# Sliding-window attention and an MLP on one core: key and value tiles 64 tokens off the query tiles

## The chip, the cores and the metric

The kernel runs on one core of one Trainium2 chip. The metric is the device time of one execution in microseconds. Three executions of the kernel before took 310.89, 311.5 and 312.32 us (median 311.5).

## The reference

Eight batches of eight heads, 576 tokens, head size 64. Each query sees itself and the 127 tokens before it, with a bias that falls linearly with the distance (ALiBi). Then comes a layer norm, an MLP with 2048 hidden units, and a residual. All inputs and the output are float32.

```python
window = 128
scores = scale * np.matmul(q, k.transpose(0, 1, 3, 2))
bias = slopes[:, None, None] * (-np.abs(rel).astype(np.float32))[None, :, :]
mask = (rel >= 0) & (rel < window)
scores = np.where(mask, scores + bias[None], -1000000000.0)
attn = softmax(scores)                      # max taken off, sum + 1e-9
x = np.matmul(attn, v)                      # -> (batch, seq, 512)
xn = (x - mu) / np.sqrt(var + 1e-06) * g_ln
out = x + np.maximum(xn @ w_ch1, 0.0) @ w_ch2
```

## The kernel before

**Blocks.** The batches are taken in four pairs (p = 0 to 3). A pair has nine blocks of 128 queries: blocks 0 to 7 are 128-token tile i = blk // 2 of batch blk % 2, and block 8 (T, the tail) holds the last 64 tokens of both batches. Block n of the whole order is p * 9 + blk, 36 in all.

**Attention of a block.** `load_qk` and `load_v` fetch queries, keys and values with POOL's DMAs, which turn float32 into float16. `turn` brings queries and keys into head-size-on-rows form: for pair 0 and the first two tiles of pair 1 with TensorE transposes (L304) and copies on DVE and ACT, from tile (1, 2) on with SP's DMA transposes (L325). Query rows are put in an order of evens first, which `store` undoes with two DMAs (L936) for each block. `attend` (L412) makes the scores with keys as the stationary side: for each pair of heads hp, each key tile (the block's own and the one before) and each head j, two products with 64 keys each in 64x64 tiles of the array (L439). `seen` cuts them to the queries that see anything, so that of two products one has 128 columns and the other 64. Four heads go to one of the two score buffers (two banks each, one for each j). ACT takes the exponential of the whole buffer, seen or not (L448, 128x1024), and DVE multiplies with a mask that holds the decay (L459; `m_full` for ordinary blocks, `m_ends` and `m_tail` for the tail, which is scored by two calls and a third, `scores_tail`). `values` multiplies the weights with the values in full 128x128 products of 65 columns (L492: 64 values and a column of ones for the sum), four heads to a bank, and divides (L500, L501).

**From block to MLP.** `stats` (DVE, POOL) and `normal` (L531) give a centred and scaled block, which SP's DMA transpose (L539) turns into `xT`. Groups of two blocks (the first six) and of four (the last six) pass `mlp1` (L740, evictions with ReLU on ACT, L756) and `mlp2` (L773) or, from group 6 on, `fast_mlp2` (L839), which uses seven products of quarters instead of eight, with sums made by DVE.

**Order.** The order on every engine is written out by hand. `steps` is a list of attention work: for block n >= 8, values of n, scores of n + 2, then statistics and masks, loads up to block n + 8, and turns of a later tile. `weave_at` runs the units of an MLP product and puts the next steps behind the units whose numbers it is given; the kernel's end lists them for each group. PE, ACT, DVE, POOL and SP each work through their own queue in that order. `decay` fills a mask with eight exponentials on ACT (L119). The products of MLP, values and turns share four PSUM banks, which from group 6 on are a `ring`.

Of the kernel before, what the change touches and what calls it, by code (L numbers as in the profile page):

```python
# [27 lines left out]

NV = 10
BY_DMA_TURN = (1, 2)  # L30
AHEAD = 8
# [8 lines left out]
def distances():  # L40

    key = np.arange(P)[:, None]
    query = np.arange(P)[None, :]

    def far(rel, ok=True):
        return np.where(ok & (rel >= 0) & (rel < WINDOW), rel, FAR)

    ends = [far(P + query - HALF * b - key, query // HALF == b) for b in range(2)]
    tail = far(query - key, query // HALF == key // HALF)
    evens_first = np.r_[0:P:2, 1:P:2]
    both = [far(P + query - key), far(query - key)]
    cols = [m[:, evens_first] for m in both] + [*ends, tail]
    return np.concatenate(cols, axis=1).astype(np.float16)


@with_exitstack
def kernel(  # L60
# [21 lines left out]
    def pool(name, bufs, **kw):  # L82
# [18 lines left out]
    dist_dram = nc.inline_tensor(distances(), name="distances")  # L101
    dist = consts.tile([P, 5 * P], FP16)
    nc.sync.dma_start(out=dist, in_=dist_dram.ap())
# [23 lines left out]
    nc.sync.dma_start(out=g_sb, in_=moe_g_ln.rearrange("(kb p) -> p kb", p=P))  # L127
    QF, QD = NFB // 2, DM // 2
    hsum = [consts.tile([P, QF, 2 * P], FP16, name=f"hs{i}", tag=f"hs{i}") for i in range(2)]
    g_line, g_row = (  # L130
        t.rearrange("p f d -> p (f d)")[:, 0 : 2 * DM].bitcast(FP32) for t in hsum
    )
    g_line = g_line[0:1]
# [75 lines left out]

    def by_dma(p, i):  # L210
        return (p, i) >= BY_DMA_TURN

    def load_qk(src, tag, p, i):

        n = min(P, S - i * P)
        t = raw_pool.tile([P, H, 2, D], FP16, tag=tag, name=tag)
        raw[tag, p, i] = t
        if by_dma(p, i):
            t = raw[tag, p, i] = t.rearrange("p h r d -> p (h r d)").rearrange(
                "p (b h d) -> p b h d", b=2, h=H  # L220
            )
            for b in range(2):
                rows = src[2 * p + b, :, i * P : i * P + n, :]
                if i == 4:
                    parts = [(t[b * n : (b + 1) * n, 0], rows)]
                elif tag == "k":
                    parts = [(t[:, b], rows)]
                else:
                    rows = rows.rearrange("h (c r) d -> h r c d", r=2)
                    parts = [  # L230
                        (t[r * HALF : (r + 1) * HALF, b], rows[:, r]) for r in range(2)
                    ]
                for dst, part in parts:
                    nc.gpsimd.dma_start(out=dst, in_=part.rearrange("h p d -> p h d"))  # L234
            return
        for b in range(2):
# [7 lines left out]
    def load_v(p, blk):  # L244
        vx = vext[(p * NSLOT + blk) % NV]
        for b, t0, n, p0 in spans(p, blk):
            nc.gpsimd.dma_start(  # L247
                out=vx[p0 : p0 + n, :, 0:D],
                in_=v[b, :, t0 : t0 + n, :].rearrange("h p d -> p h d"),
            )  # L250
# [6 lines left out]
    for n, (p, blk) in enumerate(order):  # L257
        for src, tag in ((q, "q"), (k, "k")):
            sooner = tag == "q" and 0 < blk < T and by_dma(p, blk // 2)
            if blk % 2 == 0 and not sooner:  # L260
                loads.append((load_qk, src, tag, p, blk // 2))
# [48 lines left out]
    def turn(p, i, in_sc=False, copies=(nc.vector.tensor_copy, nc.scalar.copy)):  # L310
# [3 lines left out]


        k = keys_tile("k", p, i)
        q = queries(p, i) if i < 4 else keys_tile("q", p, i)
        if by_dma(p, i):
            for tag, dst in (("q", q), ("k", k)):
                src = raw.pop((tag, p, i))  # L320
                for b in range(2 if i < 4 else 1):
                    t = dst[:, b]
                    if tag == "q" and i < 4:
                        t = turned["q", p, i][:, b].rearrange("p h r c -> p h (r c)")
                    nc.sync.dma_start_transpose(  # L325
                        out=t, in_=src[:, b].rearrange("p h d -> p (h d)")
                    )
            return
        ps = [bank(b if in_sc else None) for b in range(2)]
# [21 lines left out]
    def queries(p, i):  # L351
        if by_dma(p, i):
            t = turned_pool.tile([P, 2, HP, 2, HALF], FP16, tag="q", name="q")
            turned["q", p, i] = t
            return t
        t = turned_pool.tile([P, 2, 2, HP, HALF], FP16, tag="q", name="q")
        turned["q", p, i] = t.rearrange("p b r h c -> p b h r c")
        return t

    def keys_tile(tag, p, i):  # L360
        t = turned_pool.tile([P, 2, HP, P], FP16, tag=tag, name=tag)
        turned[tag, p, i] = t
        return t
# [34 lines left out]
    def seen(p, blk, o, t, whole):  # L398


        both, every = slice(0, 2), slice(0, HALF)
        first, second = slice(0, HALF // 2), slice(HALF // 2, HALF)
        if whole or p == 0 and blk < SEEN:
# [51 lines left out]

    def masks(p, blk, n=3):
# [21 lines left out]
    def values(p, blk, hg):  # L478
# [10 lines left out]
        for i in range(4):  # L489
            h = 4 * hg + i  # L490
            for n, (pr, t, o) in enumerate(terms):
                nc.tensor.matmul(  # L492
                    ps[:, i, :],
                    pr[:, h, t, :],
                    vext[(p * NSLOT + o) % NV][:, h, :],
                    start=(n == 0),
                    stop=(n == len(terms) - 1),
                )
        rec = small.tile([P, 4], FP32, tag="rec", name="rec")
        nc.vector.reciprocal(out=rec, in_=ps[:, :, D])  # L500
# [133 lines left out]
    def scores_step(n):  # L634
        return [(scores,) + order[n]]
# [4 lines left out]
    def values_steps(n):  # L640
        p, blk = order[n]
        return [
            [(masks, p, blk), (values, p, blk, 0)],
# [283 lines left out]
    def store(p, blk, o, cols=slice(0, DM), queues=(nc.sync,)):  # L927
        queues = cycle(queues)
        for b, t0, w, p0 in spans(p, blk):
            dst, src = out[b, t0 : t0 + w, cols], o[p0 : p0 + w, cols]  # L930
            if blk == T:
                next(queues).dma_start(out=dst, in_=src)
# [25 lines left out]
    with tc.manual_schedule(engines={engine.PE, engine.SP, engine.Pool}):  # L958
        with tc.manual_schedule(engines={engine.Activation, engine.DVE}):
# [52 lines left out]
```

## Time and profile before

| what | value |
|---|---|
| median of three runs | 311.5 us |
| the profiled execution | 308.64 us |
| its span, first to last instruction | 306.9 us |
| scores L439, products | 1088: 568 of 128 columns, 520 of 64 |
| values L492, products | 544, 65 columns, mean 193 ns |
| MLP L740, products of 512 columns | 384, mean 379 ns |
| granted TensorE clock | 0.999 |

PE is the profile's TensorE, PEld its weight loads; DVE, ACT, POOL and SP are the vector, scalar, GpSimd and sync engines. A product's own duration in the profile runs from its start to a modelled end and overlaps with the next ones: 512 columns are given 379 ns, but 32 of them, from 136.59 to 143.51 us, take 216 ns each. So what a group of products costs is read from the start of the group to the start of the next one.

### The profile page before, as it was taken

To read this page: it belongs to the slowest core of one execution; us is meant where nothing else is said; L and a number is where in the kernel's file an instruction comes from. 1 tells how busy PE (TensorE), PEld (TensorE's weight loads), DVE (VectorE), ACT (ScalarE), POOL (GpSimd) and SP (SyncE) were. 2 spreads that over 40 slices of the span, in tenths; PEclk is the share of its full clock that TensorE was granted. 3 is DMA by queue.
4 is the path that set the end of the run, shared out by engine and by line. 5 is a ranking of instruction groups with operands and counts; after the bars stand their busy time and mean duration, and the time that the engine had idled before them with its cause. 6 is when DMAs were issued, how large, how long until landed. Compare 5 with 4: busy or idle time off the path is not lost.

```text
span 306.9 us, 9072 instructions
## 1 busy us (share of the span) xinstructions
PE 297.2 (97%) x3747; PEld 200.5 (65%) x3747; DVE 220.6 (72%) x533; ACT 171.2 (56%) x297; POOL 150.6 (49%) x210
## 2 busy tenths in 40 slices
PE   8989999999999999899999999999999999999994
PEld 2468755766858576445875687568656865784583
DVE  2679877868696887737994799479948984761363
ACT  7588774757748467278247724772486257305600
POOL 8933658682399988617685657517310231000001
PEclk9999999999999999999999999999999999999999
DMA  9999999999999999999999999998845062025004
GB/s 111 159 207 201 188 167 170 202 116 117 112 100 162 149 146 139 169 151 150 88 141 183 211 88 138 134 204 65 126 88 106 17 129 47 18 45 111 0 2 137
DMA packets 150843, 38.28 MB, mean 125 GB/s; under 512 B 141809, under 2 KB 146417, under 8 KB 150802
## 3 DMA queue, kind: packets, MB, share of 16 engines
q0 software_dynamic: 103808, 18.49, 89.2%
q1 hardware_dynamic: 46594, 18.76, 37.3%
q8 instruction: 29, 0.48, 0.7%
q10 hardware_dynamic: 400, 0.46, 0.5%
q14 instruction: 12, 0.10, 0.1%
HBM read 36.90 MB, written 9.44 MB: 151 GB/s over the span
## 4 chain that ended last, share of the span: by engine, by line
PE 88%; ACT 4%; DVE 4%; DMA 3%; issue 0%; DVEq 0%
PE ps_r L740 27%; PE ps_r L839 24%; PE ps_m L773 12%; PE ps_m L740 10%; PE ps_sc L439 5%; PE ps_r L492 3%; DMA xT<-xc 3%; ACT probs L448 2%; PE ps_pv L492 2%; PE ps_warm L286 2%; PE ps_sc L304 1%; DVE o L857 1%; PE ps_tx L584 1%; DVE x L501 1%; PE ps_tr L304 0%; ACT k L337 0%
## 5 line engine op out<-in xcount | busy, mean ns | idle before, releaser
L740 PEld LDWEIGHTS <-w1g 128*128 128x128 f16 x640 | 61.0, 98 | 49.8 <-issue 2.9
L740 PE MATMUL ps_r<-xT,w1g 128*128 128x512 f16 x384 | 84.8, 379 | 1.3 <-DMA xT<-xc 1.3
L448 ACT ACTIVATE probs<-ps_sc 128x1024 f16<-128x1024 f32 x56 | 54.2, 1026 | 56.0 <-PE ps_sc L439 56.0
L756 ACT ACTIVATE ht<-ps_r 128x512 f16<-128x512 f32 x96 | 56.1, 599 | 33.3 <-PE ps_r L740 33.1
L544 POOL TENSOR_TENSOR rstd<-moments,powers 128x1 f32<-128x1 f32 x28 | 14.1, 502 | 93.2 <-DVE moments L590 93.2
L773 PE MATMUL ps_m<-w,ht 128*128 128x512 f16 x192 | 45.5, 380 | 0.0
L839 PE MATMUL ps_r<-w,ht 128*128 128x256 f16 x384 | 43.9, 273 | 0.0
L839 PEld LDWEIGHTS <-ht 128*128 128x128 f16 x384 | 37.2, 98 | 4.7
L247 POOL DMA_DIRECT2D vx<-in_v_dram x40 | 34.9, 879 | 8.3 <-DVE probs L459 2.1
L756 ACT ACTIVATE ht<-ps_m 128x256 f16<-128x256 f32 x91 | 33.3, 389 | 7.5 <-PE ps_m L740 4.6
L459 DVE TENSOR_TENSOR probs<-probs,m 128x1024 f16<-128x1024 f16 x56 | 35.7, 675 | 2.0 <-ACT probs L448 2.0
L234 POOL DMA_DIRECT2D q<-in_q_dram x46 | 31.8, 702 | 2.4 <-DMA q<-in_q_dram 1.1
L740 PE MATMUL ps_m<-xT,w1g 128*128 128x256 f16 x256 | 30.4, 273 | 0.7 <-ACT ht L756 0.6
L773 PEld LDWEIGHTS <-ht 128*128 128x128 f16 x192 | 17.3, 98 | 18.0
L589 DVE BATCH_NORM_STATS2 st<-x 128x6 f32<-128x512 f16 x36 | 24.8, 688 | 0.7
L547 POOL TENSOR_TENSOR rstd<-rstd,powers 128x1 f32<-128x1 f32 x28 | 22.7, 812 | 2.2
L500 DVE RECIPROCAL rec<-ps_r 128x4 f32<-128x4 f32 x36 | 6.3, 176 | 23.9 <-PE ps_r L492 23.8
L234 POOL DMA_DIRECT2D k<-in_k_dram x26 | 22.3, 867 | 0.6 <-PE ps_m L740 0.5
L839 PE MATMUL ps_r<-w,hs 128*128 128x256 f16 x192 | 21.9, 273 | 0.0
L492 PEld LDWEIGHTS <-probs 128*128 128x128 f16 x448 | 18.7, 97 | 4.6 <-DVE probs L459 0.3
L439 PE MATMUL ps_sc<-q,k 64*64 64x128 f16 (+1 forms) x1088 | 19.9, 208 | 1.5 <-ACT probs L448 1.0
L857 DVE TENSOR_TENSOR o<-ps_r,o 128x512 f32<-128x512 f32 (+1 forms) x25 | 16.6, 666 | 5.5 <-PE ps_r L839 5.1
(87 smaller groups left out, 359.0 us busy)
## 6 DMA issues: line engine op xcount, KB each, us to landing
out_dram<-o SPq DMA_DIRECT2D x66, 128.0 KB, 4.2
k<-in_k_dram POOLq DMA_DIRECT2D x32, 128.0 KB, 6.3
vx<-in_v_dram POOLq DMA_DIRECT2D x32, 128.0 KB, 8.1
w<-in_moe_w_ch_dram POOLq DMA_DIRECT2D x8, 512.0 KB, 11.2
q<-in_q_dram POOLq DMA_DIRECT2D x48, 64.0 KB, 6.6
q<-in_q_dram POOLq DMA_DIRECT2D x12, 128.0 KB, 4.7
k<-in_k_dram POOLq DMA_DIRECT2D x8, 64.0 KB, 5.2
vx<-in_v_dram POOLq DMA_DIRECT2D x8, 64.0 KB, 4.5
```

The source lines that it names most:

```text
L234: nc.gpsimd.dma_start(out=dst, in_=part.rearrange("h p d -> p h d"))
L247: nc.gpsimd.dma_start(out=vx[p0 : p0 + n, :, 0:D], in_=v[b, :, t0 : t0 + n, :].rearrange("h p d -> p h d"),)
L439: nc.tensor.matmul(in_halves(ps[cols, j, n, t, :])[:, r, queries], kt[rows, hp, cols], in_halves(qt[rows, b, hp])[:, r, queries], start=Tr ...
L448: nc.scalar.activation(out=dst.rearrange("p (n j) q -> p j n q", j=2), in_=ps.rearrange("p j n t q -> p j n (t q)"), func=AF.Exp, scale=in ...
L459: nc.vector.tensor_tensor(out=dst, in0=dst, in1=mask, op=ALU.mult)
L492: nc.tensor.matmul(ps[:, i, :], pr[:, h, t, :], vext[(p * NSLOT + o) % NV][:, h, :], start=(n == 0), stop=(n == len(terms) - 1),)
L547: nc.gpsimd.tensor_tensor(out=here, in0=here, in1=powers[:, 1:2], op=ALU.pow)
L589: nc.vector.bn_stats(out=st, in_=xs[order[n]])
L740: nc.tensor.matmul(ps[:, 0:cols], w[:, kb, fb * P : (fb + 1) * P], xT[:, kb, 0:cols], start=(kb == 0), stop=(kb == NKB - 1),)
L756: nc.scalar.activation(out=ht[:, fb, 0:cols], in_=ps[:, 0:cols], func=AF.Relu)
L773: nc.tensor.matmul(sums[at], ht[:, fb, at * P : (at + 1) * P], w2[:, fb, :], start=(fb == 0), stop=(fb == NFB - 1),)
L839: nc.tensor.matmul(banks[name][pair][:, pair, :], lhs[:, fb, pair * P : (pair + 1) * P], rhs[:, fb, :], start=(first and fb == 0 and (pair ...
```

## The change

From pair 1 on (`LATE = 1`):

- Key and value tiles begin 64 tokens off the query tiles: tile 0 holds tokens 0 to 63 of a batch, tile i tokens 128 i - 64 to 128 i + 63. All 128 queries of a tile see some part of the middle tile; the first half of the queries sees also the second half of the tile before, and the second half the first half of the tile after. The window thus is one 128x128 piece and two 64x64 corners. `FIRST_ROWS` and `LAST_ROWS` are the two halves of the rows, `BEYOND` the columns 128 to 191.
- `attend_late` makes the corners with 64x64 tiles (64 queries) and the middle piece with 64x128 tiles (128 keys, 128 queries); four heads fill 768 columns instead of 1024. Block T is scored in two calls instead of three, and `scores_tail` is left for pair 0 alone.
- `values_late` takes the eight heads together: first the middle piece of all, then the corners, added into the same sums; then `divide`, which is the old end of `values`.
- Every tile of the late pairs is turned by DMA, keys one tile ahead of queries; queries stay in their natural order, so a tile's queries are loaded with two DMAs instead of four and a block is stored with one instead of two.
- A new mask `m_late`, filled by `decay` in the middle of `mlp1(2)`, serves all late blocks; `m_full` and `m_ends` share the memory of `hsum`. There are 12 value tiles instead of 10, five turned key tiles instead of four, three turned query tiles instead of four.
- The places of the steps in `mlp1(5)` change.

```diff
-NV = 10
-BY_DMA_TURN = (1, 2)
+NV = 12
+LATE = 1
...
+    low, high = key < HALF, key >= HALF
+    outer = far(np.where(low, query - key, query + P + HALF - key), query < HALF)
+    cols += [far(query + HALF - key), outer[:, :HALF]]
...
-    m_full, m_ends = (
-        consts.tile([P, H, 2 * P], FP16, name=f"m{i}", tag=f"m{i}") for i in range(2)
-    )
+    QF, QD = NFB // 2, DM // 2
+    hsum = [consts.tile([P, QF, 2 * P], FP16, name=f"hs{i}", tag=f"hs{i}") for i in range(2)]
+    m_full, m_ends = hsum
+    m_late = consts.tile([P, H, P + HALF], FP16)
...
+            t0 = i * P - HALF * (tag == "k" and i > 0)
+            half = i == (0 if tag == "k" else 4)
-                rows = src[2 * p + b, :, i * P : i * P + n, :]
-                if i == 4:
-                    parts = [(t[b * n : (b + 1) * n, 0], rows)]
-                elif tag == "k":
-                    parts = [(t[:, b], rows)]
+                if half:
+                    dst, n = t[b * HALF : (b + 1) * HALF, 0], HALF
                 else:
-                    rows = rows.rearrange("h (c r) d -> h r c d", r=2)
-                    parts = [
-                        (t[r * HALF : (r + 1) * HALF, b], rows[:, r]) for r in range(2)
-                    ]
-                for dst, part in parts:
-                    nc.gpsimd.dma_start(out=dst, in_=part.rearrange("h p d -> p h d"))
+                    dst, n = t[:, b], P
+                nc.gpsimd.dma_start(
+                    out=dst, in_=heads_last(src[2 * p + b, :, t0 : t0 + n, :])
+                )
...
+    def v_at(p, o):
+        return vext[(p * NSLOT + o + max(p - LATE, 0)) % NV]
+
+    def load_v(p, o):
+        vx = v_at(p, o)
+        if p < LATE:
+            parts = spans(p, o)
+        elif o < 2:
+            parts = [(2 * p + o, 0, HALF, HALF)]
+        else:
+            parts = [(2 * p + o % 2, o // 2 * P - HALF, P, 0)]
...
+        i, odd = divmod(blk, 2)
+        late = p >= LATE
+        if not odd:
+            if not late or i == 0:
+                loads.append((load_qk, q, "q", p, i))
+            if not late or blk < T:
+                loads.append((load_qk, k, "k", p, i + late))
+            if blk == T and LATE <= p + 1 < NPAIR:
+                loads.append((load_qk, k, "k", p + 1, 0))
         loads.append((load_v, p, blk))
-        if blk % 2 and blk < T - 1 and by_dma(p, blk // 2 + 1):
-            loads.append((load_qk, q, "q", p, blk // 2 + 1))
+        if late and blk == T:
+            loads.append((load_v, p, T + 1))
+        if late and odd:
+            loads.append((load_qk, q, "q", p, i + 1))
...
+            todo = [("q", p, i)] + [("k", p, i + 1)] * (i < 4)
+            if (i == 0 and p == LATE) or (i == 4 and p + 1 < NPAIR):
+                todo.append(("k", p + (i == 4), 0))
+            for tag, p, i in todo:
+                src, dst = raw.pop((tag, p, i)), keys_tile(tag, p, i)
+                for b in range(1 if i == (0 if tag == "k" else 4) else 2):
+                    nc.sync.dma_start_transpose(
+                        out=dst[:, b], in_=src[:, b].rearrange("p h d -> p (h d)")
+                    )
+            return
...
+        t = turned_pool.tile([P, 2, 2, HP, HALF], FP16, tag="q", name="q", bufs=3)
+            [P, 2, HP, P], FP16, tag=tag, name=tag, bufs=3 if tag == "q" else 5
...
-        if o == blk:
-            return [(0, both, every), (1, both, second)]
-        return [(1, both, every), (0, both, first)]
...
+    def key_tile(p, b, o):
+        t = turned["k", p, o]
+        return t[:, 0, :, b * HALF : (b + 1) * HALF] if o == 0 else t[:, b]
+    def attend_late(p, blk, hps):
+        i, b = divmod(blk, 2)
+        heads = slice(2 * hps[0], 2 * hps[-1] + 2)
+        width = 2 * P if blk == T else P if i == 0 else P + HALF
+        if hps[0] == 0:
+            if i == 0:
+                pr = own_pool.tile([P, H, 1, P], FP16, tag="own", name="own")
+            else:
+                pr = probs_pool.tile([P, H, 2, P], FP16, tag="probs", name="probs")
+            pr = pr.rearrange("p h t q -> p (h t q)")[:, 0 : H * width]
+            weights_of[p, blk] = pr = pr.rearrange("p (h c) -> p h c", h=H)
+        else:
+            pr = weights_of[p, blk]
+        at = len(scored) % 2
+        scored.append((p, blk))
+        ps = ps_sc[at][:, :, 0 : len(hps) * width].rearrange("p j (n c) -> p j n c", c=width)
+        qt = turned["q", p, i]
+        def products(part):
+            for n, hp in enumerate(hps):
+                for dst, col, o, keys, bq, queries in part:
+                    for j in range(2):
+                        rows = slice(j * HALF, (j + 1) * HALF)
+                        nc.tensor.matmul(
+                            ps[dst, j, n, col : col + queries.stop - queries.start],
+                            key_tile(p, bq, o)[rows, hp, keys],
+                            qt[rows, bq if blk < T else 0, hp, queries],
+                            start=True,
+                            stop=True,
+                        )
+        every, low, high = slice(0, P), FIRST_ROWS, LAST_ROWS
+        if blk == T:
+            mine = [(c, slice(c * HALF, (c + 1) * HALF)) for c in range(2)]
+            outer = [(high, P + c * HALF, 3, high, c, qs) for c, qs in mine]
+            inner = [(every, c * HALF, 4, every, c, qs) for c, qs in mine]
+        elif i == 0:
+            outer = [(low, 0, 1, low, b, high)]
+            inner = [(high, 0, 0, low, b, every)]
+        else:
+            outer = [(high, P, i - 1, high if i > 1 else low, b, low)]
+            outer += [(low, P, i + 1, low, b, high)]
+            inner = [(every, 0, i, every, b, every)]
+        products(outer)
+        products(inner)
+        dst = pr[:, heads]
+        nc.scalar.activation(
+            out=dst.rearrange("p (n j) c -> p j n c", j=2),
+            in_=ps,
+            func=AF.Exp,
+            scale=inv_sqrt_d,
+        )
+        m = m_late[:, heads]
+        if blk == T:
+            todo = [
+                (
+                    dst[:, :, x * P : (x + 1) * P].rearrange("p h (b c) -> p h b c", b=2),
+                    m[:, :, x * P : x * P + HALF].unsqueeze(2).broadcast_to([P, 4, 2, HALF]),
+                )
+                for x in range(2)
+            ]
+        elif i == 0:
+            todo = [(dst[high], m[high, :, 0:P]), (dst[low, :, 0:HALF], m[low, :, BEYOND])]
+        else:
+            todo = [(dst, m)]
+        unmasked.setdefault((p, blk), []).extend(todo)
...
+        if p >= LATE:
+            for hps in [every] if blk < 2 else [low, high]:
+                attend_late(p, blk, hps)
...
+    def values_late(p, blk):
+        n = p * NSLOT + blk
+        if n % 2 == 0:
+            x_pairs[n // 2] = x_pool.tile([P, 2, DM], FP16, tag="x", name="x")
+        xs[p, blk] = x_pairs[n // 2][:, n % 2, :]
+        i, b = divmod(blk, 2)
+        pr = weights_of.pop((p, blk))
+        every, low, high = slice(0, P), FIRST_ROWS, LAST_ROWS
+        if blk == T:
+            mine = [slice(c * HALF, (c + 1) * HALF) for c in range(2)]
+            inner = [(qs, every, qs, T + c) for c, qs in enumerate(mine)]
+            outer = [
+                (qs, high, slice(P + c * HALF, P + (c + 1) * HALF), T - 2 + c)
+                for c, qs in enumerate(mine)
+            ]
+        elif i == 0:
+            inner = [(every, high, every, b)]
+            outer = [(high, low, slice(0, HALF), 2 + b)]
+        else:
+            inner = [(every, every, every, blk)]
+            outer = [(low, high, BEYOND, blk - 2), (high, low, BEYOND, blk + 2)]
+        ps = [
+            psum("ps_pv")[:, 0 : 4 * (D + 1)].rearrange("p (h d) -> p h d", h=4)
+            for _ in range(2)
+        ]
+        for part in (inner, outer):
+            for hg in range(2):
+                for h in range(4):
+                    for dst, keys, queries, o in part:
+                        nc.tensor.matmul(
+                            ps[hg][dst, h, :],
+                            pr[keys, 4 * hg + h, queries],
+                            v_at(p, o)[keys, 4 * hg + h, :],
+                            start=part is inner and h == 0,
+                            stop=part is outer,
+                            skip_group_check=True,
+                        )
+        for hg in range(2):
+            divide(p, blk, hg, ps[hg])
+    def divide(p, blk, hg, ps):
...
+        if p >= LATE:
+            return [[(masks, p, blk), (values_late, p, blk)], []]
...
-    steps += [values_steps(6)[1], x_step(6) + masks_of(7), variance_of(5)]
+    steps += [values_steps(6)[1], x_step(6) + masks_of(7), variance_of(5) + [(decay, m_late, 5)]]
     steps += [*values_steps(7), x_step(7) + variance_of(6)]
-    steps += [turn_step(8) + variance_of(7), scores_step(8) + turn_step(9)]
+    steps[-1] += turn_step(9)
+    steps += [turn_step(8) + variance_of(7), scores_step(8) + turn_step(11)]
...
-            if by_dma(order[m][0], order[m][1] // 2) == (m == n + 4)
+            if (order[m][0] >= LATE) == (m == n + 4)
-    steps.append(turn_at(8))
+    steps.append([])
-        if n + 1 < count and order[n + 1][1] == T:
-            step += [(scores_tail, order[n][0])]
...
-            if blk == T:
+            if blk == T or p >= LATE:
...
-            weave_at(mlp1(5), 0, 5, 5, 8, 10, 12, also=(3, 6, 9))
+            weave_at(mlp1(5), 0, 4, 4, 6, 8, 10, also=(3, 7, 11))
```

More of the change, by code (lines that the diff above doesn't have):

```diff
@@ L101 @@
     dist_dram = nc.inline_tensor(distances(), name="distances")
-    dist = consts.tile([P, 5 * P], FP16)
+    dist = consts.tile([P, 6 * P + HALF], FP16)
     nc.sync.dma_start(out=dist, in_=dist_dram.ap())
@@ L127 @@
     nc.sync.dma_start(out=g_sb, in_=moe_g_ln.rearrange("(kb p) -> p kb", p=P))
[L128 to L132, printed above, removed]
+    spread = hsum[1].rearrange("p f d -> p (f d)").bitcast(FP32)
+    g_line, g_row = spread[:, 0:DM], spread[:, DM : 2 * DM]
     g_line = g_line[0:1]
@@ L208, with heads_last @@
     raw = {}
-    def by_dma(p, i):
-        return (p, i) >= BY_DMA_TURN
+    def heads_last(rows):
+        return rows.rearrange("h p d -> p h d")
     def load_qk(src, tag, p, i):
-        n = min(P, S - i * P)
         t = raw_pool.tile([P, H, 2, D], FP16, tag=tag, name=tag)
         raw[tag, p, i] = t
-        if by_dma(p, i):
+        if p >= LATE:
             t = raw[tag, p, i] = t.rearrange("p h r d -> p (h r d)").rearrange(
@@ L242, in load_qk @@
             )
-    def load_v(p, blk):
-        vx = vext[(p * NSLOT + blk) % NV]
-        for b, t0, n, p0 in spans(p, blk):
+    def v_at(p, o):
[8 more added lines that the diff above has]
+            parts = [(2 * p + o % 2, o // 2 * P - HALF, P, 0)]
+        for b, t0, n, p0 in parts:
             nc.gpsimd.dma_start(
-                out=vx[p0 : p0 + n, :, 0:D],
-                in_=v[b, :, t0 : t0 + n, :].rearrange("h p d -> p h d"),
+                out=vx[p0 : p0 + n, :, 0:D], in_=heads_last(v[b, :, t0 : t0 + n, :])
             )
@@ L257 @@
     for n, (p, blk) in enumerate(order):
[L258 to L261, printed above, removed]
+        i, odd = divmod(blk, 2)
[7 more added lines that the diff above has]
+                loads.append((load_qk, k, "k", p + 1, 0))
         loads.append((load_v, p, blk))
-        if blk % 2 and blk < T - 1 and by_dma(p, blk // 2 + 1):
-            loads.append((load_qk, q, "q", p, blk // 2 + 1))
+        if late and blk == T:
+            loads.append((load_v, p, T + 1))
+        if late and odd:
+            loads.append((load_qk, q, "q", p, i + 1))
         place.append(len(loads))
@@ L310, in turn @@
     def turn(p, i, in_sc=False, copies=(nc.vector.tensor_copy, nc.scalar.copy)):
+        if p >= LATE:
[9 more added lines that the diff above has]
+            return
         k = keys_tile("k", p, i)
         q = queries(p, i) if i < 4 else keys_tile("q", p, i)
[L318 to L328, printed above, removed]
         ps = [bank(b if in_sc else None) for b in range(2)]
@@ L360, in keys_tile @@
     def keys_tile(tag, p, i):
-        t = turned_pool.tile([P, 2, HP, P], FP16, tag=tag, name=tag)
+        t = turned_pool.tile(
+            [P, 2, HP, P], FP16, tag=tag, name=tag, bufs=3 if tag == "q" else 5
+        )
         turned[tag, p, i] = t
@@ L402, in seen @@
         first, second = slice(0, HALF // 2), slice(HALF // 2, HALF)
-        if whole or p == 0 and blk < SEEN:
+        if whole or blk < SEEN:
             return [(0, both, every), (1, both, every)]
@@ L454, in attend @@
         unmasked.setdefault((p, blk), []).append((dst, mask[:, heads, :]))
-    def masks(p, blk, n=3):
+    FIRST_ROWS, LAST_ROWS = slice(0, HALF), slice(HALF, P)
+    BEYOND = slice(P, P + HALF)
+    def key_tile(p, b, o):
[65 more added lines that the diff above has]
+        unmasked.setdefault((p, blk), []).extend(todo)
@@ L457, in masks @@
+    def masks(p, blk, n=4):
         todo = unmasked.get((p, blk), [])
@@ L463, in scores @@
         low, high, every = [0, 1], [2, 3], [0, 1, 2, 3]
-        if blk == T:
+        if p >= LATE:
+            for hps in [every] if blk < 2 else [low, high]:
+                attend_late(p, blk, hps)
+        elif blk == T:
             attend(p, T, [6, 7], m_ends, "probs", low)
```

12 lines of the change are left out of this document (5 added, 7 removed).

## The prediction

> **What bounds the kernel now.** I read the page first (span, busy shares, chain), then the stages, then TensorE's instructions in order of time, where the starts of neighbouring groups give prices that the mean durations hide.
>
> ```profile
> span 306.9 us, 9072 instructions
> PE 297.2 (97%) x3747; PEld 200.5 (65%) x3747; DVE 220.6 (72%) x533; ACT 171.2 (56%) x297; POOL 150.6 (49%) x210
> PE 88%; ACT 4%; DVE 4%; DMA 3%; issue 0%; DVEq 0%
> ```
>
> PE is busy for 97% of the span and is 88% of the chain. The busy time of each engine by stage:
>
> ```profile
> 75.00:129.00 54.00, 51.93 (x713) 36.28 (x707) 42.12 (x101) 32.56 (x63) 40.93 (x56) 1.00 1.64 138
> 129.00:245.00 116.00, 116.00 (x1356) 79.24 (x1355) 90.21 (x198) 64.57 (x93) 55.21 (x76) 1.00 1.44 126
> ```
>
> From 129 us on PE (second figure) is never idle, with DVE at 90.2 and ACT at 64.6 of 116 us. So whatever PE issues more or less there goes into the time one for one, and work saved on the other engines goes nowhere. Before 129 us there are a few waits. PE in order of time, in four places of the dense stages (start, duration, line, tiles, count):
>
> ```profile
> 151.33 0.65 PE L492 MATMUL ps_r<-vx,probs 128*128 128x65 f16 x16
> 151.91 0.54 PE L439 MATMUL ps_sc<-q,k 64*64 64x128 f16 x32
> 152.39 1.92 PE L839 MATMUL ps_r<-w,w 128*128 128x256 f16 x16
> ...
> 182.21 0.45 PE L439 MATMUL ps_sc<-q,k 64*64 64x64 f16 x32
> 182.58 0.28 PE L839 MATMUL ps_r<-w,w 128*128 128x256 f16 x1
> ...
> 256.54 0.32 PE L439 MATMUL ps_sc<-q,k 64*64 64x64 f16 x16
> 256.79 0.39 PE L740 MATMUL ps_r<-xT,w1g 128*128 128x512 f16 x1
> ...
> 263.70 0.23 PE L492 MATMUL ps_r<-vx,probs 128*128 128x65 f16 x2
> ...
> 264.43 0.82 PE L839 MATMUL ps_r<-w,ht 128*128 128x256 f16 x6
> ```
>
> Start to start: the 24 value products at 263.70 hand over to another 128x128 product after 0.73 us, 30.4 ns each. The 16 at 151.33 should take 0.487, but the 64x64 scores start after 0.58: **0.093 us goes into the change of tile shape**. Scores of 64 columns take 0.25 for 16 and 0.37 to 0.38 for 32, so 16 cost 0.126 (four in 31.5 ns) and about 0.125 is fixed: 0.025 for a slower first four, 0.10 for the change back. A visit to 64x64 tiles thus costs 0.12 going in and 0.10 coming out. An ordinary block (2 to 7) costs 0.58 + 0.48 = 1.06 us, in two changes of shape.
>
> **The change on PE.** The late pairs have 27 blocks: 18 ordinary, 6 first ones (blocks 0 and 1) and 3 tails. I write X for a change between two small shapes (64x64 with 64x128 or 128x64), which no row shows.
>
> Ordinary block, before: 32 score products, half of 128 columns, half of 64. After: 16 corners of 64 columns in 64x64 (four side by side, 31.5 ns) and 8 of 128 columns in 64x128. Per set of heads that is 192 columns in both versions, so no streaming is saved. The values go from 16 products to 8 full ones and 16 corners in 64x64. After: own keys 8 x 30.3 ns = 0.242; change 0.12; corners as 8 pairs x 31.5 ns = 0.252; scores twice (corners 2 x 31.5 ns = 0.063, full keys 2 x 56 ns = 0.112), the 56 being half of the 109 ns between L740's starts with 256 columns; change back 0.10. Sum 1.07 + 3X: corners to full keys, to corners, to full keys. Against 1.06: +0.012 + 3X, times 18: **+0.2 + 54X**.
>
> First blocks: values were 8 products (0.24, and 0.12 to go to the scores); now 8 of 64x128 in one row half, then 8 corners in a single quarter: 0.12 + 0.242 + X + 0.252, so +0.24 + X. Scores have the same 16 products, but corners and own keys now share half of the array and run after one another, 4 x 31.5 + 4 x 56 = 0.35 instead of 0.22: +0.1. Times 6: **+2.0 + 6X**.
>
> Tails: scores 0.606 + 3X against 0.354, and the 16 of the tail (0.126, in the last pair 0.25 with its own changes) go away; values 16 of 128x64 in pairs and 16 corners in pairs, 0.744 against 0.845 (in the last pair 0.1 more for the way out). Over the three: **+0.3 + 9X**.
>
> Turns: two turns by PE (L304, 64 products each) leave, 0.69 and 0.88 us from the starts around 67.5 and 72.3 us: **-1.6**.
>
> So PE gets +0.97 + 69X. **X** is bounded below by 0 (the rows of the array stay in halves of 64) and above by 0.12 (going in from 128x128). I take 0.093, the bare handover measured at 151.91, as the nearest row: 69 x 0.093 = 6.4.
>
> The Trainium skill, TensorEngine Tiling (Array Packing), Key Properties, says that a change of tiling mode, not of the tile alone, drains TensorE; 64x64 and 64x128 are different modes in its list. The 0.093 us agrees for 128x128 to 64x64, and no run here shows the other pairs. By that rule X is not 0, which speaks against this change.
>
> **The other engines.** On the path only before 129 us:
>
> ```profile
> L448 ACT ACTIVATE probs<-ps_sc 128x1024 f16<-128x1024 f32 x56 | 54.2, 1026 | 56.0 <-PE ps_sc L439 56.0
> L756 ACT ACTIVATE ht<-ps_r 128x512 f16<-128x512 f32 x96 | 56.1, 599 | 33.3 <-PE ps_r L740 33.1
> L119 ACT ACTIVATE m<-dist 128x256 f16<-128x256 f16 x16 | 5.1, 408 | 1.0 <-DMA dist<-distances 1.0
> 111.63 2.34 PE L740 MATMUL ps_m<-xT,w1g 128*128 128x256 f16 x20 [0.29 <-ACT ht L756]
> 128.86 0.81 PE L740 MATMUL ps_r<-xT,w1g 128*128 128x512 f16 x3 [1.32 <-DMA xT<-xc]
> ```
>
> Exponentials: 768 instead of 1024 elements. Busy over count is 0.97 us for 1024 and 0.58 for 512, so 0.78: 0.39 less per block. Behind them PE lost time three times: the stretches of L740 from 97.74, 109.42 and 114.77 take 2.65, 4.39 and 3.57 us where 109 ns each make 2.18, 3.92 and 3.05: 0.47 + 0.47 + 0.52 = 1.46. Most of 0.39 comes back each time: **-1.15** (bounds -1.46 and 0).
>
> The wait at 128.86: the last piece of xT is issued by SP at 120.97 and lands 7.75 us later (chain). The new weave puts its block two units earlier, SP has one store less per block, and PE has more between. **-1.2** (bounds -1.38 and 0).
>
> The new decay m_late: 8 activations of 192 columns, about 0.265 each between 0.21 (128) and 0.32 (256): 2.1 us on ACT, put behind the fourth unit of mlp1(2) at 57.5 us. ACT's idle gaps there are 0.2 to 0.7 us, and queued behind are the evictions (L756) that PE's four banks wait for. The next eviction starts at 59.6 instead of 58.0, and the eighth unit, at 59.0 now, needs its bank: **+1.1** (bounds 0 and 2.1).
>
> At nothing: masks (L459) shrink by a quarter, or go from 3 to 4 instructions in the tail, under DVE's 26 us of slack in the steady stage. POOL issues 20 fewer query loads of 0.70 us and SP 24 fewer stores of 0.6; neither bounds. SP gets nine transposes for the first two tiles of pair 1 (1.25 to 1.8 us each, 5 to 7 us to land). SP has only 12 stores between 46 and 76 us, so the first five go out from about 57 and land by 69 or 70, when PE wants them (scores at 69.98); if they are late, up to 2 us. Scores and values now need keys and values one tile further on, but loads are issued 8 blocks ahead. The divisions of the first four heads come 0.5 us later, two banks being held at once; the bank is wanted again only two units (1.7 us) later.
>
> **Sum.** 0.97 + 6.4 - 1.15 - 1.2 + 1.1 = +6.1 us. The profiled execution took 308.64 (span 306.9 and 1.7 around it), so 314.8; the runs shown have a median of 311.5, 2.9 above it, and the forecast in their terms is 311.5 + 6.1 = **317.6**. With X between 0.06 and 0.12 it is 315.3 to 319.5, the forecast's own range.
>
> **Rivals.** A difference within 0.5% (1.6 us) can't be told from none.
>
> (a) No price between small shapes, X = 0: 0.97 - 1.15 - 1.2 + 1.1 = -0.3, 311.2. For it: both shapes split the rows in the same halves. Against it: the only changes seen cost 0.09 to 0.12. Chance 0.23.
>
> (b) Faster: the relief of ACT and SP between 57 and 129 us, in full. All 1.46 behind ACT and all 1.38 behind xT go, and the banks cover m_late: 0.97 - 2.84 = -1.9 plus 69X, 309.6 at X = 0. It decides for faster while 69X stays under 0.3 us, X below 5 ns. For it: those waits are in the trace and lie on the paths that the change relieves. Against it: the small room on ACT at 57 us, and X. Chance 0.20.
>
> (c) Products meant to run in pairs do not: the value corners of the two row halves write the same bank, while the side-by-side scores of L439 write one bank for each row half. 8 x 31.5 ns more for 18 blocks: +4.5, 322.1 with the forecast's X, 315.7 without. Chance 0.12.
> The Trainium skill, TensorEngine Tiling, Gotcha 1, says that different row tiles can't access one PSUM bank at the same time; no run here shows such a pair. By that rule (c) would hold.
>
> Forecast: 0.45. Over the cases: faster 0.18 of (b) and 0.04 of (a) = 0.22; within 0.5% 0.17; slower 0.61. The range is 309.3 to 322.0, from a little below (b) to (c).
>
> **What would show it.** Right: from 129 us PE still has no idle time, an ordinary block costs about 1.35 us start to start instead of 1.06, and a gap near 0.09 us stands at each step from corners to full keys. Wrong by X: that gap is no larger than the 31 ns of the product before it. (c): value corners 31 ns apart instead of in pairs. The side terms: PE's waits at 100, 111 and 117 us and at 128 us gone, a wait of about 1 us near 59. A wait for q or k near 70 us, or for xT after 129, would be something I have priced at nothing.

## The result and the profile after

The changed kernel takes 319.62 us (median of six runs, 316.77 to 321.97), the kernel before beside it 311.56. The ratio on record is 1.0278 with a 95% interval of 1.0233 to 1.0324 (the quotient of these two medians is 1.026): slower by 2.8%, where 317.6 us (309.3 to 322.0) was forecast.

The profiled execution on record took 321.97 us and was held up more than the others. So the stages are read from a second profile of the same kernel, taken in the first experiment (c0_after, 318.46 us). First the page of the one on record (span, busy shares, chain), then the stages of the second (start and end, length, busy time of PE, PEld, DVE, ACT and POOL, clock, DMA share, GB/s).

```profile
span 320.2 us, 8826 instructions
PE 308.4 (96%) x3643; PEld 205.1 (64%) x3643; DVE 217.2 (68%) x540; ACT 162.0 (51%) x298; POOL 138.0 (43%) x190
...
PE 82%; DMA 9%; DVE 5%; ACT 1%; POOL 1%; issue 1%; SPq 0%; DVEq 0%; POOLq 0%
```

```profile
75.00:129.00 54.00, 54.00 (x696) 37.40 (x695) 39.57 (x99) 28.63 (x61) 39.55 (x52) 1.00 1.99 156
129.00:245.00 116.00, 116.00 (x1303) 75.19 (x1302) 83.79 (x191) 59.20 (x91) 49.95 (x67) 1.00 1.32 130
```

PE issues 104 products fewer and is busy 11 us longer. ACT is relieved by 9 us, POOL by 13 and DVE by 3, and none of it helps: from 129 to 245 us PE is still never idle, at the full clock, and it starts 1303 products there where it started 1356.

An ordinary block in that stage, in the second profile: values, the corners of values and scores mixed, then the rest of the scores, then the next full product.

```profile
162.49 0.73 PE L624 MATMUL ps_r<-vx,probs 128*128 128x65 f16 x20
163.03 0.22 PE L502 MATMUL ps_sc<-q,k 64*64 64x64 f16 x2
...
163.12 0.84 PE L502 MATMUL ps_sc<-q,k 64*64 64x64 f16 x20
163.90 1.47 PE L878 MATMUL ps_r<-xT,w1g 128*128 128x512 f16 x6
```

From 162.49 to 163.90 it is 1.41 us, against 1.06 before. The last 20 score products alone take 0.78 us. That is where the time went.

The same stretch product by product, start to start: from the last corner of the scores to the first full key 125 ns pass (124 to 126 in all 28 such places of the stage), where the next group of corners would follow after 32. So the bare step is 0.093 us. Behind it the first pair of full keys takes 66 ns to the next pair (in c1 below, later pairs take 56), and on the way back the first four corners take 52 instead of 32.

The stage from the first 512-column product (L740) to the last product of the kernel took 174.00 us before (128.86 to 302.86) and 180.70 in both profiles after. This **dense stage** repeats to 0.02 us in every kernel below that has the same products in it, so it serves as the ruler: +6.70 us of the 8. The rest lies before it.

### The profile page after: what moved, and what is told of

It is laid out like the page before. It is cut to its first block, busy times and chain, and to the rows that moved or that the text cites. A ratio compares the mean times of both kernels' runs of the same rounds, so it can differ in the third digit from the quotient of the medians.

```text
span 320.2 us, 8826 instructions
## 1 busy us (share of the span) xinstructions
PE 308.4 (96%) x3643; PEld 205.1 (64%) x3643; DVE 217.2 (68%) x540; ACT 162.0 (51%) x298; POOL 138.0 (43%) x190
## 4 chain that ended last, share of the span: by engine, by line
PE 82%; DMA 9%; DVE 5%; ACT 1%; POOL 1%; issue 1%; SPq 0%; DVEq 0%; POOLq 0%
PE ps_r L878 26%; PE ps_r L977 23%; PE ps_m L911 10%; PE ps_m L878 9%; PE ps_sc L502 5%; PE ps_r L624 3%; DMA xT<-xc 3%; DMA k<-k 2%; DMA vx<-in_v_dram 2%; DMA k<-in_k_dram 2%; DVE w1g L165 2%; PE ps_pv L624 1%; PE ps_warm L300 1%; PE ps_sc L448 1%; PE ps_pv L585 1%; DVE st L726 1%
## 5 line engine op out<-in xcount | busy, mean ns | idle before, releaser
L894 ACT ACTIVATE ht<-ps_r 128x512 f16<-128x512 f32 x96 | 57.3, 598 | 36.2 <-PE ps_r L878 35.9
L525 ACT ACTIVATE probs<-ps_sc 128x768 f16<-128x768 f32 (+1 forms) x42 | 33.0, 838 | 61.3 <-PE ps_sc L502 61.3
L681 POOL TENSOR_TENSOR rstd<-moments,powers 128x1 f32<-128x1 f32 x28 | 11.6, 414 | 109.4 <-DVE moments L727 109.3
L878 PE MATMUL ps_m<-xT,w1g 128*128 128x256 f16 x256 | 31.3, 280 | 3.4 <-DMA xT<-xc 2.7
L230 POOL DMA_DIRECT2D k<-in_k_dram x30 | 26.1, 875 | 13.1 <-DMA k<-k 11.1
L230 POOL DMA_DIRECT2D q<-in_q_dram x30 | 25.5, 855 | 2.8 <-DMA vx<-in_v_dram 2.8
L502 PE MATMUL ps_sc<-q,k 64*64 64x64 f16 (+3 forms) x624 | 23.3, 206 | 0.2 <-DMA k<-k 0.2
L549 DVE TENSOR_TENSOR probs<-probs,m_late 128x768 f16<-128x768 f16 (+1 forms) x48 | 22.1, 507 | 0.0
L684 POOL TENSOR_TENSOR rstd<-rstd,powers 128x1 f32<-128x1 f32 x28 | 20.6, 735 | 2.2
L977 PEld LDWEIGHTS <-hs 128*128 128x128 f16 x192 | 18.8, 98 | 2.2
```

Of the source, the lines that this page charges most:

```text
L230: nc.gpsimd.dma_start(out=dst, in_=heads_last(src[2 * p + b, :, t0 : t0 + n, :]))
L502: nc.tensor.matmul(ps[dst, j, n, col : col + queries.stop - queries.start], key_tile(p, bq, o)[rows, hp, keys], qt[rows, bq if blk < T els ...
L525: nc.scalar.activation(out=dst.rearrange("p (n j) c -> p j n c", j=2), in_=ps, func=AF.Exp, scale=inv_sqrt_d,)
L684: nc.gpsimd.tensor_tensor(out=here, in0=here, in1=powers[:, 1:2], op=ALU.pow)
L878: nc.tensor.matmul(ps[:, 0:cols], w[:, kb, fb * P : (fb + 1) * P], xT[:, kb, 0:cols], start=(kb == 0), stop=(kb == NKB - 1),)
L894: nc.scalar.activation(out=ht[:, fb, 0:cols], in_=ps[:, 0:cols], func=AF.Relu)
```

## The experiments

Theory "shapes": each change between 64x64 and 64x128 tiles costs PE about 0.1 us. Theory "feeding": the time goes into loads and transposes that come late before 129 us. Ratios are to the kernel before on the same chip.

### c0_after: the changed kernel again

> The changed kernel once more, as the reference for the others on the same chip, and for a second look at its waits before 129 us. Theory 'shapes' (each change between 64x64 and 64x128 tiles costs PE about 0.1 us, 69 of them, 6 to 7 of the 8 us): the dense stage repeats to 0.1 us, an ordinary block takes 1.40 us from its values to the next full product, against 1.05 before. Theory 'feeding' (the time goes into late loads and transposes: PE waits 2.7 us for xT at 95 us, and the clock falls after it): that wait is there again and is 2 us or more. Ratio to before 1.028 by both.

Ratio 1.0234 (1.0149 to 1.032). The dense stage was 180.70 us again. The wait at 95 us was not there: PE is busy for all 54 us between 75 and 129. "Feeding" as the main cause falls here, since the wait that it rests on differs from one execution of the kernel to the next, and this execution is 6.70 us longer in the dense stage all the same.

### c1_corners_first: one change of shape in the scores instead of three

```diff
         products(outer)
+        yield
         products(inner)
...
-            for hps in [every] if blk < 2 else [low, high]:
-                attend_late(p, blk, hps)
+            parts = [attend_late(p, blk, hps) for hps in ([every] if blk < 2 else [low, high])]
+            for _ in range(2):
+                for part in parts:
+                    next(part, None)
```

> Only the order of the score products of a late block changes: the corners of both sets of heads, then the middle pieces of both, so one change of shape inside the scores instead of three; the same 24 products. Shapes: two changes less in 21 blocks, 0.095 to 0.105 us each, 4.0 to 4.4 us less than the changed kernel, ratio to before about 1.014. Feeding, or any theory that counts products or columns: the same time as the changed kernel within 0.5 us, ratio 1.028.

Ratio 1.0132 (1.0057 to 1.0207), 315.04 us against 317.91 of c0 on the same chip. The same products in another order, PE in order of time:

```profile
162.85 0.73 PE L627 MATMUL ps_r<-vx,probs 128*128 128x65 f16 x20
...
163.48 0.62 PE L502 MATMUL ps_sc<-q,k 64*64 64x64 f16 x20
164.03 2.33 PE L881 MATMUL ps_r<-xT,w1g 128*128 128x512 f16 x10
```

A block takes 1.18 us (162.85 to 164.03), and the last 20 products 0.55 instead of 0.78: 0.23 for two changes. The dense stage is 177.53 us, 3.17 less. Fourteen blocks with two sets of heads are scored in it, so 28 changes went, **0.113 us each**. Nothing but the order differs, so a theory that counts products or columns falls. The whole kernel gained 2.9 us against c0, less than the 4.0 to 4.4 expected: before the dense stage this profile has PE waiting 1.5 us for keys at 70 us and 2.2 us at 94, which c0's has at 0.7 and not at all.

### c2_all_64: all score products in 64x64 tiles

```diff
-                for dst, col, o, keys, bq, queries in part:
+                for dst, col, o, keys, bq, queries in [
+                    (slice(d.start + c, d.start + c + HALF), col, o,
+                     slice(ks.start + c, ks.start + c + HALF), bq, qs)
+                    for d, col, o, ks, bq, qs in part
+                    for c in range(0, d.stop - d.start, HALF)
+                ]:
```

> The middle piece of the scores is made by two products of 64 keys instead of one of 128, so that all score products of a block have 64x64 tiles: 32 products an ordinary block instead of 24, no change of shape inside the scores. Shapes: 63 of the 69 changes go, about 0.3 us in each of 21 blocks, 6.0 to 6.6 us less, ratio to before 1.007 to 1.009. A theory by which the number of products or of weight loads costs: slower than the changed kernel, by up to 168 x 4 to 8 ns = 1.3 us. Feeding: no difference within 0.5 us.

Ratio 1.0116 (1.0032 to 1.02), 314.73 us. PE in order of time:

```profile
162.46 0.73 PE L629 MATMUL ps_r<-vx,probs 128*128 128x65 f16 x20
...
163.09 0.52 PE L507 MATMUL ps_sc<-q,k 64*64 64x128 f16 x28
163.53 2.76 PE L883 MATMUL ps_r<-xT,w1g 128*128 128x512 f16 x12
```

28 products now take 0.44 us where 20 took 0.78, and the block is back at 1.07 us. The dense stage is 176.09 us, 4.61 less for 42 changes: **0.110 us each**. More products, less time. The whole kernel gained 3.2 us against c0 instead of the 6.0 expected: 4.6 in the dense stage, and some given back before it, where this profile has PE waiting at 95 us and again for xT at 131.

### c3_five_raw_keys: a fifth buffer for loaded keys

```diff
-        t = raw_pool.tile([P, H, 2, D], FP16, tag=tag, name=tag)
+        t = raw_pool.tile([P, H, 2, D], FP16, tag=tag, name=tag, bufs=5 if tag == "k" else 4)
```

> One more buffer for loaded keys (five instead of four), nothing else. Feeding: the key load that POOL holds back from 62 to 73 us goes out at once, the burst of loads after 73 us is gone, PE's wait of 2.7 us for xT at 95 us falls under 1 us and the clock stays near 1.00, 2 to 4 us less where the wait was, ratio to before 1.015 to 1.022. Rival: the wait comes from the nine extra DMA transposes on SP and not from POOL, then it stays at 2 us or more. Shapes has nothing to gain here; the dense stage keeps 1.40 us a block.

Ratio 1.0228 (1.0146 to 1.031), the time of c0. The longest wait on POOL, in the changed kernel on record and then here (total, times, longest):

```profile
POOL k L230 <- DMA k<-k: 11.1, 1, 11.1
```

```profile
POOL k L230 <- DMA k<-k: 1.7, 1, 1.7
```

The wait of POOL is a consequence of the change, as keys are now loaded one tile ahead of the queries. It went with the fifth buffer, and the time didn't follow. The wait for xT at 94 us was 0.35 us here, under 1 us as "feeding" had it, but c0 had none there without the buffer. A miss for "feeding" by this path; that the loads held back were not yet due would fit, but was not followed up.

### d1_before_turns: the two turns alone, in the kernel before

```diff
-BY_DMA_TURN = (1, 2)
+BY_DMA_TURN = (1, 0)
...
-    steps += [turn_step(8) + variance_of(7), scores_step(8) + turn_step(9)]
+    steps[-1] += turn_step(9)
+    steps += [turn_step(8) + variance_of(7), scores_step(8) + turn_step(11)]
...
-    steps.append(turn_at(8))
+    steps.append([])
```

> The kernel before with one part of the change alone: tiles 0 and 1 of pair 1 are turned by SP's DMA transposes instead of TensorE (128 products of L304 and eight copies leave; eight transposes of 128 KB come). Tiles of keys, scores and values as before. The prediction's step 'turns' stands for -1.6 us; if the transposes land after about 70 us PE waits for them and up to 2 us are given back. Shapes: 1.0 to 1.6 us less, ratio 0.995 to 0.997. Feeding (transposes and loads crowd each other before 100 us): PE waits for q, k or xT between 68 and 100 us, ratio 1.00 to 1.01.

Ratio 0.9995 (0.9965 to 1.0026): nothing gained. PE reaches the values of block 11 at 88.49 us, 1.5 earlier than before, and then:

```profile
91.57 0.60 PE L741 MATMUL ps_m<-xT,w1g 128*128 128x256 f16 x4 [0.98 <-DMA xT<-xc]
```

It waits 0.98 us for xT, and again 1.1 at 128 us. The transposes say why. The xT that PE waits for at 91 us was issued 1.4 us earlier than before (85.31 instead of 86.75), but took 6.1 us to land instead of 4.9. The turned keys between 55 and 100 us took longer too, from issue to landing, before and then here:

```profile
DMA to landing us min/median/max: 3.5/4.8/5.5
```

```profile
DMA to landing us min/median/max: 5.0/7.2/10.9
```

SP issues the transposes of keys, queries and xT alike, and with eight more of them both kinds landed later. From 75 to 85 us, before and here, the DMA share (last figure but one; the time of all transfers against that of the 16 DMA engines, it can pass 1) is 0.82 and 1.80:

```profile
75.00:85.00 10.00, 10.00 (x129) 8.03 (x123) 7.09 (x19) 7.56 (x16) 2.58 (x4) 1.00 0.82 110
```

```profile
75.00:85.00 10.00, 10.00 (x111) 7.46 (x109) 6.64 (x17) 6.51 (x15) 4.18 (x7) 1.00 1.80 182
```

### d2_before_turns_places: with the new places in mlp1(5) too

> As d1, and with the places of the steps in mlp1(5) that the changed kernel has. If the prediction's reading of the wait for xT at 128 us is right (the last block of the group comes two units too late), most of its 1.3 us go: 0.8 to 1.3 us less than d1, ratio to before 0.991 to 0.994. If the wait follows the load on SP and the DMA engines instead of the places, it stays and the time is d1's.

Ratio 0.999 (0.9962 to 1.0017). The time is d1's: 0.4 us less by the medians, where 0.8 to 1.3 was expected. The wait at 128 us is gone, as the places would have it. In this profile PE waits 3.0 us for xT at 91 us instead, and the 44 products after that take 7.57 us instead of 4.80, with the granted clock at 0.74 between 95 and 105 us. The profiled execution took 312.59 us, 2.7 above the median, so that wait may be longer here than it mostly is. What the places are worth stays open: in e1 and e3 below the wait at 128 us goes with the old places.

### d3_all_64_mended and d4_decay_later

d3 is c2 and c3 together with the filling of m_late moved; d4 is the changed kernel with that step alone moved:

```diff
-    steps += [values_steps(6)[1], x_step(6) + masks_of(7), variance_of(5) + [(decay, m_late, 5)]]
+    steps += [values_steps(6)[1], x_step(6) + masks_of(7), variance_of(5)]
...
-    steps.append([])
+    steps.append([(decay, m_late, 5)])
```

> The changed kernel with all score products in 64x64 tiles, m_late filled one stage later where ACT is idle (about 73 us), and a fifth buffer for loaded keys. Shapes: the 0.11 us for each change of shape seen in the two runs above explains all but some 2 us, so this lands 0.9 us under the run with 64x64 alone, ratio to before 1.004 to 1.010. It beats the kernel before only if the waits before 129 us were worth more than PE's products say. If the number of products mattered (they are 32 a block as before, and 24 instead of 16 for the values), it stays at 1.012 or above.

> The changed kernel with one step moved: m_late is filled after the scores of block 9 (about 73 us, inside mlp2(2)) instead of inside mlp1(2). The prediction's step 'decay' was +1.1 us there; the changed kernel shows a stall of PE of 0.7 to 0.9 us at 61 us behind ACT's evictions. Expected: that stall gone, 0.6 to 0.9 us less than the changed kernel, ratio to before about 1.021 to 1.024. Rival: the time is passed on to the next wait before 129 us (for xT or k) and the kernel's time does not move.

d3: 1.0112 (1.0084 to 1.0141), with 176.09 us in the dense stage and PE waiting 2.1 us for turned keys at 70 us; above the range expected. d4: 1.0274 (1.0228 to 1.032), no gain. The stall behind the evictions was real, as the changed kernel on record shows:

```profile
61.80 1.03 PE L878 MATMUL ps_m<-xT,w1g 128*128 128x256 f16 x8 [0.73 <-ACT ht L894]
```

It is gone in d4, but there PE waits 2.4 us for turned keys, where the profile on record has 0.2:

```profile
72.82 0.41 PE L502 MATMUL ps_sc<-q,k 64*64 64x128 f16 x8 [2.42 <-DMA k<-k]
```

The rival named for d4 held: before 129 us PE runs up against the transposes, and time saved ahead of them is not kept.

### e1 to e4: loads six blocks ahead instead of eight

```diff
-        return [(load_until, place[min(n + AHEAD, count - 1)])]
+        return [(load_until, place[min(n + (AHEAD if n < 2 else 6), count - 1)])]
```

e1 is d1 with this line, e2 is d2 with it, e3 the kernel before, e4 is d3.

> The kernel before with the two turns by DMA (as d1) and with loads issued six blocks ahead instead of eight from the third block on. In d1 the 1.6 us that PE saved came back as waits for xT at 91 us (1.0) and 128 us (1.1), while the transposes of keys took 7.2 us to land instead of 4.8. Feeding, by loads: with fewer loads in flight between 60 and 100 us the transposes land sooner, the wait at 91 us falls under 0.3 us, 1 to 1.6 us less than d1, ratio 0.994 to 0.997. Rival: SP's queue (eight more transposes of 1.3 to 1.7 us each before xT's) is what delays xT, then the wait at 91 us stays and the ratio is 0.998 to 1.002.

> As e1, with the places of the steps in mlp1(5) from the changed kernel (as d2). If the loads were the cause, the wait at 91 us and the one at 128 us are both gone: 2 to 2.8 us less than before, ratio 0.991 to 0.994, under both kernels. If SP's queue is the cause: the 91 us wait stays, ratio 0.997 to 1.001.

> The kernel before with loads six blocks ahead from the third block on, nothing else: the control of e1 and e2. Expected the same as before within 0.3% by both readings (its only wait for xT, 1.3 us at 128 us, may move by up to 1 us either way); slower only if a load now comes too late, which would show as PE waiting for q, k or v.

> The mended form of the changed kernel (d3: all score products 64x64, m_late filled later, five key buffers) with loads six blocks ahead from the third block on. d3 lost 2.1 us in the dense stage, which stays (176.1 us against 174.0 before), and 2.1 us waiting for turned keys at 70 us. Feeding, by loads: that wait halves at least, ratio 1.004 to 1.008. By SP's queue: it stays, ratio 1.010 to 1.013.

| kernel | median, us | ratio | 95% interval |
|---|---|---|---|
| before | 309.86 | | |
| e1 | 307.28 | 0.9906 | 0.9876 to 0.9936 |
| e2 | 307.72 | 0.9919 | 0.9888 to 0.9949 |
| e3 | 309.41 | 0.9964 | 0.9937 to 0.9991 |
| e4 | 311.90 | 1.0073 | 1.0043 to 1.0102 |

**e1 and e2 beat both kernels**, by 0.8 to 0.9% of the kernel before. The control moved too: e3 is at 0.9964, a little beyond the 0.3% expected, and has no wait at 128 us. So that wait goes with the loads, and some 0.4% comes from the loads alone. e1 differs from e3 by the two turns alone and lies 2.1 us under it, about the 1.6 us that the turns took off PE. Not quite as expected, though: the wait at 91 us stays in e1 (and at 0.7 us in e2), and is put down to another engine in the same place.

```profile
91.52 0.71 PE L741 MATMUL ps_m<-xT,w1g 128*128 128x256 f16 x5 [0.91 <-DVE o L918]
```

It is xT still. The xT that PE needs there was issued at 85.34 us and landed at 91.38, as in d1 (85.31 and 91.43), and PE starts 0.14 us after it in both; DVE's `o` ended at 91.40, within 0.02 us of it, but in the kernel before PE starts this product at 91.89 with that `o` not begun (92.09), so it doesn't need it. Fewer loads left this landing and the turned keys (7.1 us, 7.2 in d1) where they were, and the wait stayed as the rival, SP's queue, had it, though not the time. The other transposes of xT did gain: between 70 and 100 us the median is 5.5 us instead of 7.5 in d1. That SP's queue makes the remaining 0.9 us was not tried by a run of its own. e4 keeps 176.11 us in the dense stage, and its wait for keys at 70 us falls from 2.1 to 0.8: as "feeding, by loads" had it. The tiles 64 tokens off stay slower than the kernel before even so.

## Why the prediction was right, step by step

**What bounds.** Right: PE, one for one, from 129 us on. The dense stage changed only with the products in it.

**The time.** 319.62 us lies in the range, which says little, as that runs from faster to slower; it is 2.0 above the forecast and just past the forecast's own 315.3 to 319.5. Of the 2.0, 0.85 are missing in the dense stage (6.70 us, where 1.57 + 46 x 0.093 = 5.85 follows from the steps below) and 1.1 before it.

**The sum of the products.** Right. An ordinary block was 1.07 + 3X, and 1.41 makes X 0.113. With X left open, the steps give for the dense stage 12 ordinary blocks, 4 first ones by their values and 2 by their scores, and 2 tails: 1.57 + 46 X us. The 6.70 us measured make X 0.112, and c2, in which only 4 X are left, should show 1.57 + 0.45 = 2.0 and shows 2.09.

**X.** The mechanism held and the size was low: 0.110 to 0.113 us instead of 0.093. The bare step came out at 0.093 us, as taken. What this price leaves out is what the prediction had itself listed for the way into small tiles, a slower first group: 0.010 us more into full keys and 0.020 into corners, which makes 0.103 and 0.113. The upper bound, 0.12, was the nearer one. 69 times the difference is 1.2 to 1.4 us. This is the term that was mis-sized. The rule of the Trainium skill, TensorEngine Tiling (Array Packing), Key Properties, that a change of mode drains TensorE, thus agrees with this case for a change that leaves the rows in halves of 64, at 0.11 us.

**Turns, -1.6.** The products left PE, the gain did not reach the end: d1 is 0.9995. The step failed as a net term. It took time saved before 129 us as saved, while the landing of xT set the pace at 91 and 128 us, and came later with the transposes that took PE's place.

**ACT, -1.15.** Right as to its place: the second profile keeps 0.16 us of the 1.46, at 121 us. In c1, where PE's blocks are shorter, 0.34 us of waiting behind ACT is back there. **xT at 128 us, -1.2.** Gone in the changed kernel, as forecast, but back at 1.4 us in c2 and 1.2 in d3, which have the new places and the fewer stores too but a faster PE: so of the three reasons given, the last one, that PE has more between, is the one that the runs bear out. **m_late, +1.1.** 0.73 us by the trace, and nothing when it was moved (d4). **At nothing.** The transposes for pair 1 were late, as allowed for: PE waited 0.2 us at 72 us in the profile on record, 2.4 in d4. POOL's wait of 11 us was not foreseen, and cost nothing that c3 could measure.

**Rivals.** (a), no price for the change of shape, fell with c1 and c2. (b), relief of ACT and SP, fell with X. (c) fell in the changed kernel's own trace: from 162.49 to 163.03 lie 8 full products (0.24), the change (0.12) and 12 corners, which have 0.18 us left, 30 ns for two. One after another, at 31.5 ns, the 12 alone would take 0.38. They run in pairs though both write one bank, to different partitions. The sentence of the Trainium skill, TensorEngine Tiling (Array Packing), Gotcha 1, against one bank for two row tiles is thus not borne out here for halves that write different partitions.

## What to carry to other kernels

Count the changes of tile shape on TensorE before the products: at 0.11 us, one change here cost as much as some fourteen products of 64x64 with 64 columns (8 ns each, four side by side). So group products by shape, or split the larger ones. Relieving engines that were off the bound by 9 and 13 us bought nothing. Time that PE saved ahead of a stretch paced by transfers was kept here only with fewer loads in flight: the two turns are worth nothing in d1 and about 0.6% between e3 and e1.

## What the hardware showed besides

A wait of PE is paid twice when it is long enough. In the changed kernel on record:

```profile
98.18 6.34 PE L878 MATMUL ps_m<-xT,w1g 128*128 128x256 f16 x44 [2.68 <-DMA xT<-xc]
```

The 44 products after a wait of 2.68 us take 6.2 us start to start instead of 4.8: half speed for the first 2.7 us. In c1 a wait of 2.17 us was followed, after four products, by sixteen at half speed, and in d4 the wait of 2.42 us was followed by half speed too; in d3 one of 2.1 us left the clock at 1.00.

The first product of the MLP (L740) starts at 19.3 to 20.0 us in nine of the profiles and at 20.8 to 21.3 in five others, with no regard to the kernel: 19.4 before, 21.2 and 21.3 in the two profiles of the changed kernel, 19.6 in c3. A difference of two profiles of one execution each holds up to 2 us of this.
